# Three edits at the two ends of a fused attention and feed-forward kernel: q's first load in two requests, two constants in one, one store per last tile

## The chip, the cores and the metric

The kernel runs on one core of a Trainium2 chip. The metric is the device time of one launch in microseconds: 280.95 us, the median of 3 runs (280.93 to 281.48). The engines are named as the profile names them: PE is TensorE's matmul stream, PEld its weight loads, DVE is VectorE, ACT is ScalarE, POOL is GpSimd, SP is SyncE. SP, ACT and POOL can issue DMA requests; the requests are carried out by 16 DMA engines that all three share.

## What is computed

Linear attention with cosine weights for 8 batches of 8 heads (576 tokens, 64 features per head), and then a two-layer product with the gate h cos h over all 4608 tokens. From the reference:

```python
r = np.maximum(x, 0.0)                                  # x is q or k
phi = np.concatenate([r * c, r * s], axis=-1)           # c, s: cos and sin of (pi/2) * pos / 576
kv  = np.einsum('bhsf,bhsd->bhfd', k_p, v);  z = np.sum(k_p, axis=2)
num = np.einsum('bhsf,bhfd->bhsd', q_p, kv)
den = np.einsum('bhsf,bhf->bhs', q_p, z)[..., None] + 1e-06
x = (num / den).transpose(0, 2, 1, 3).reshape(4608, 512)
h = x @ w_in                                            # 512 x 2048
g = h * np.cos(h)
out = g @ w_out                                         # 2048 x 512, float32
```

## The kernel before

The 4608 tokens are worked on in nine chunks of 512. Eight batches give 576 tokens each: 512 of them make the batch's own chunk, and the 64 left over of every batch together make the ninth chunk, numbered 8. So the last chunk's four tiles of 128 tokens each hold 64 tokens of an even batch (partitions 0 to 63) and 64 tokens of the odd batch after it (partitions 64 to 127).

Each chunk passes through three stages: attention (load q, k, v; scale by cosines and sines; transpose; products; normalize; transpose), `layer1` (product with `w_in`, cosine, gate) and `layer2` (product with `w_out`, store). From the third chunk on `layer1` can, and `layer2` does, use a scheme of seven half-size products in place of eight, with sums formed on DVE or by DMA. `Plan.add` collects steps with their engine, cost and dependencies. The order is not worked out when the kernel is built: `STARTS` holds one planned time for each step and `ENGS` the engine, and `Plan.run` sorts the steps by the planned time. On each engine the instructions then stand in that order, and a semaphore is waited for wherever data is not there yet.

The parts of the code around the change:

- `setup` (L1025): ACT issues the load of `CS` (cosines and sines, 128 partitions of 24 floats, L1032) and then of `IDENT` (the 128 x 128 identity in float16 that PE uses for its transposes, L1033). `CS` is read by every scaling step (`prep`, L369 and L370), `IDENT` by every transpose on PE.
- `load` (L330): a batch's q, k or v comes in two parts. 320 of the tokens lie as five rows to a partition (`go5`, L337) and 256 as four rows to a partition (`go4`, L340), each on one half of the 128 partitions. SP issues these loads (`LQ`). For the first chunk the order on SP is q (four rows, five rows), k (four, five), and v in two groups of four heads (four, five, four, five). DVE and ACT scale q only after both of its parts have landed.
- `weights` (L1048): POOL copies one element of scaled q and then issues the loads of `w_in`, so that the weights do not run ahead of q, k and v.
- `layer2(8)` (L917), the last stage: sums of the earlier products are stored as they are finished, and the seventh product completes the first 256 output columns of the last two tiles; each tile is added up by DVE (L1020) and stored by `store_tile` (L859).
- `store_tile` calls `put` (L821) twice for a tile, once for each half of the partitions: the half of the even batch goes by SP, the half of the odd batch by ACT. Each request stores 64 rows of 256 floats, 64 KB. Ahead of them each of SP and ACT stores 256 KB and 128 KB of the same chunk.

At the end of the program SP waits for every store to land.

Of the kernel before, what the change touches and what calls it, by code (L numbers as in the profile page):

```python
# [17 lines left out]
OPT = dict(F16=0, WS2=[3, 1], HQ=[3, 0, 1], AQ=0, L0S=0, FW=[20, 4, 4, 4, 4], W2F=2, WQ=3, L2F=0, WFI=None,  # L18
           XPE=[0, 1, 2, 3, 4], FAST1={3: 2, 4: 2, 5: 2, 6: 4, 7: 4, 8: 4}, MODE={}, HH='', LD=[['k', 0],
           ['v', 0], ['q', 0], ['k', 1], ['v', 1], ['q', 1]], NB=[['A0', 'A1'], ['A0', 'A1', 'M0']],  # L20
           XB=[['B3'], ['B3', 'M1']], W0=5, W1=6, WF=[[2, 2, 2, 2], [2, 2, 0, 0]], HOLD=['k', 1], P0=0,
           RAW1=4, WO2=1, H1=0, DA=0, W2=0, SQ=0, NUZ=1)
# [169 lines left out]
def kernel(  # L192
# [12 lines left out]
    P = 128  # L205
# [29 lines left out]
    def sb(name, shape, dt=F16):  # L235
        return pool.tile(shape, dt, name=name)
# [1233 lines left out]
```

## Time and profile before

| what | value |
|---|---|
| median of 3 runs | 280.95 us |
| the profiled execution, whole | 282.01 us |
| span from its first instruction to its last | 280.2 us |
| instructions | 6814 |
| granted TensorE clock | 1.000 throughout |
| DMA, mean over the span | 207 GB/s |

The span is what the rows below count in; the whole time of an execution also holds what lies before and after it. The views used are: the page (busy time of each engine, the chain of waits that ended last as shares), the same chain in order of time, the timeline of instructions and DMA issues, windows (busy time of each engine in a stretch, then TensorE's clock, the share of time in which the 16 DMA engines were busy, and GB/s), the DMA view of a stretch (the share of the DMA engines in tenths and the GB/s for 40 equal slices, then the queues and the issues with the time from issue to landing) and the instructions of one tile. In the DMA view q1 is SP's queue, q10 is ACT's and q0 is POOL's. A line such as "out<-in x4: 497/558/618" gives the least, the median and the longest duration in ns.

### The profile page before, as it was taken

The page shows a single profiled execution, that of the slowest core. Times are in us where ns is not written, and L with a number is a line of the kernel's source. Part 1 is how long each engine was busy: PE and PEld are TensorE (multiplying, and loading weights), DVE is VectorE, ACT ScalarE, POOL GpSimd, SP SyncE. Part 2 cuts the span into 40 slices and gives each one's busy share as a digit, 9 for nine tenths or more (in the row PEclk, how much of TensorE's full clock was granted, in tenths as well). Part 3 has the DMA queues.
Part 4 walks back from the last instruction along what each step waited for, and adds up shares of the span by engine and source line. Part 5 has one row for each costly group of instructions (what it writes and reads, how often), then busy time and mean ns, then how long its engine had stood idle before and what let it go on. Part 6 is the DMA issues. An engine that isn't in the chain of part 4 may idle for free.

```text
span 280.2 us, 6814 instructions
## 1 busy us (share of the span) xinstructions
PE 270.6 (97%) x2689; PEld 213.9 (76%) x2689; DVE 235.3 (84%) x439; ACT 212.4 (76%) x366; POOL 83.5 (30%) x105
## 2 busy tenths in 40 slices
PE   8799999999999999999999999999999999999993
PEld 3468847788866577778777878789988888888882
DVE  1886877999999998999999998989989879873952
ACT  2847698999999896788989988995658686776330
POOL 1360010210602101530340045042534372399210
PEclk9999999999999999999999999999999999999999
DMA  6999999799999999979999998839656495698125
GB/s 201 337 195 204 291 334 310 261 271 191 321 306 244 213 250 266 284 216 227 258 265 271 209 259 282 116 92 147 157 75 144 104 156 107 151 143 123 75 77 150
DMA packets 80223, 58.03 MB, mean 207 GB/s; under 512 B 43200, under 2 KB 77248, under 8 KB 80192
## 3 DMA queue, kind: packets, MB, share of 16 engines
q1 hardware_dynamic: 68960, 39.99, 60.6%
q0 software_dynamic: 10496, 17.04, 29.0%
q10 hardware_dynamic: 736, 0.57, 0.7%
q8 instruction: 21, 0.34, 0.5%
q14 instruction: 10, 0.08, 0.1%
HBM read 36.75 MB, written 11.80 MB: 173 GB/s over the span
## 4 chain that ended last, share of the span: by engine, by line
PE 83%; DVE 7%; DMA 4%; ACT 2%; issue 1%; SPq 0%; DVEq 0%
PE M L956 32%; PE M L737 14%; PE M L576 9%; PE M L609 8%; PE TR L737 6%; PE M L881 3%; PE ATT L465 3%; PE ATT L398 3%; DMA qT<-KQ 2%; DMA qm<-in_q_dram 2%; DVE gT L550 2%; PE TR L609 2%; PE ATT L1044 1%; DVE XN L486 1%; DVE KQ L370 1%
## 5 line engine op out<-in xcount | busy, mean ns | idle before, releaser
L956 PEld LDWEIGHTS <-gT 128*128 128x128 f16 x560 | 53.8, 98 | 7.6
L956 PE MATMUL M<-w_out_sb,gT 128*128 128x256 f16 x448 | 57.0, 273 | 0.0
L550 DVE TENSOR_TENSOR gT<-M,ch 128x512 f16<-128x512 f32 x73 | 48.7, 684 | 5.2 <-ACT ch L548 5.1
L548 ACT ACTIVATE ch<-M 128x512 f32<-128x512 f32 x75 | 43.9, 596 | 12.0 <-PE M L576 6.2
L369 ACT ACTIVATE KQ<-km,CS 128x512 f16<-128x512 f32 x58 | 39.7, 719 | 0.6 <-DMA km<-in_k_dram 0.6
L967 ACT ACTIVATE ost<-M 128x512 f32<-128x512 f32 x41 | 24.4, 597 | 18.0 <-PE M L956 13.0
L369 ACT ACTIVATE KQ<-qm,CS 128x512 f16<-128x512 f32 x48 | 32.8, 718 | 4.5 <-DMA qm<-in_q_dram 4.5
L609 PE MATMUL M<-xT,w_in_sb 128*128 128x512 f16 x136 | 33.6, 379 | 0.0
L956 PE MATMUL M<-T,S 128*128 128x256 f16 x256 | 32.4, 273 | 0.0
L385 POOL CAST V<-vm 128x1024 f16<-128x1024 f32 (+1 forms) x18 | 15.8, 903 | 51.5 <-DMA vm<-in_v_dram 14.7
L737 PEld LDWEIGHTS <-w_in_sb 128*128 128x128 f16 x288 | 27.2, 98 | 4.8 <-issue 0.4
L576 PE MATMUL M<-xT,w_in_sb 128*128 128x256 f16 x256 | 30.1, 272 | 0.8 <-DVE gT L550 0.5
L576 PEld LDWEIGHTS <-w_in_sb 128*128 128x128 f16 x256 | 24.6, 97 | 5.0 <-issue 1.4
L956 PEld LDWEIGHTS <-S 128*128 128x128 f16 x256 | 24.9, 98 | 4.6 <-DVE S L932 0.2
L749 DVE TENSOR_TENSOR Z<-M,Z 128x512 f32<-128x512 f32 x31 | 21.1, 687 | 4.6 <-PE M L737 3.2
L609 PEld LDWEIGHTS <-w_in_sb 128*128 128x128 f16 x160 | 14.9, 98 | 12.4
L550 POOL TENSOR_TENSOR gT<-Z,ch 128x512 f16<-128x512 f32 x5 | 6.3, 1266 | 56.7 <-ACT ch L548 20.0
L486 DVE TENSOR_TENSOR XN<-ATT,rec 128x512 f16<-128x512 f32 x32 | 22.1, 691 | 1.1
L465 PEld LDWEIGHTS <-qT 128*128 128x128 f16 (+1 forms) x320 | 14.7, 101 | 6.0 <-issue 2.7
L745 ACT ACTIVATE Z<-M 128x512 f32<-128x512 f32 x26 | 15.1, 596 | 4.0 <-PE M L737 3.0
L760 ACT ACTIVATE ch<-Z 128x1024 f32<-128x1024 f32 x12 | 12.7, 1057 | 6.9 <-DVE Z L749 4.9
L465 PE MATMUL ATT<-kvz,qT 128*128 128x65 f16 (+1 forms) x288 | 16.1, 195 | 0.9 <-DMA qT<-KQ 0.4
(153 smaller groups left out, 512.6 us busy)
## 6 DMA issues: line engine op xcount, KB each, us to landing
out_dram<-ost POOLq DMA_DIRECT2D x38, 256.0 KB, 4.0
qm<-in_q_dram SPq DMA_DIRECT2D x8, 640.0 KB, 6.2
km<-in_k_dram SPq DMA_DIRECT2D x8, 640.0 KB, 7.1
qm<-in_q_dram SPq DMA_DIRECT2D x8, 512.0 KB, 6.4
km<-in_k_dram SPq DMA_DIRECT2D x8, 512.0 KB, 5.2
vm<-in_v_dram SPq DMA_DIRECT2D x6, 640.0 KB, 6.6
vm<-in_v_dram SPq DMA_DIRECT2D x6, 512.0 KB, 4.8
w_in_sb<-in_moe_w_in_dram POOLq DMA_DIRECT2D x4, 512.0 KB, 7.9
```

The lines of the kernel that those rows point to most:

```text
L369: fn = {"ACT": lambda: nc.scalar.activation(out=out_, in_=in_, func=AF.Relu, scale=sc), "DVE": lambda: nc.vector.tensor_scalar(out=out_, i ...
L385: "POOL": lambda: nc.gpsimd.tensor_copy(out=out_, in_=in_)}
L465: nc.tensor.matmul(bank[hb][ps, hh * D1:(hh + 1) * D1], lhsT=x[:, h, :], rhs=z[:, h, :], start=True, stop=True)
L486: nc.vector.tensor_tensor(out=split(x16[n][:, hs, :], k), in0=A[:, :, :, 0:D], in1=split(rec[n][:, hs], k).unsqueeze(3).broadcast_to((P, k ...
L548: act(0.5, due, lambda: nc.scalar.activation(out=ch[c], in_=bank, func=AF.Sin, bias=math.pi / 2.0, scale=1.0), [key], [("ch", c)])
L550: mul(due, 0.61, lambda q: q.tensor_tensor(out=dst, in0=bank if len(dst.shape) == 2 else bank.rearrange("p (j s) -> p j s", j=dst.shape[1] ...
L576: nc.tensor.matmul(M1[m][:, jj * 2 * P:(jj + 1) * 2 * P], lhsT=w_in_sb[:, cc, j * P:(j + 1) * P], rhs=X[:, cc, ts], start=(cc == 0), stop= ...
L609: nc.tensor.matmul(M, lhsT=w_in_sb[:, cc, j * P:(j + 1) * P], rhs=X[:, cc, :], start=(cc == 0), stop=(cc == NCT - 1))
L737: nc.tensor.matmul(bank[0][:, j * TH:(j + 1) * TH], lhsT=a(cc, j), rhs=b[:, cc, :], start=(first and j == 0 and cc == 0), stop=(last and j ...
L749: dve(0.61, due + 0.3, lambda: nc.vector.tensor_tensor(out=dst, in0=bank[0], in1=dst, op=ALU.add), [bank[1], key], [key])
L956: nc.tensor.matmul(bank[0][:, tt * MH:(tt + 1) * MH], lhsT=a[:, j, tt * P:(tt + 1) * P], rhs=b[:, j, :], start=(first and (apart or tt == ...
L967: act(0.5, due, lambda: nc.scalar.activation(out=dst, in_=view(bank), func=AF.Copy), [bank[1]], dk)
```

## The change

Three edits; the matmuls and the order of everything else on each engine stay as they were, and the planned times are only renumbered.

1. The four-row part of q's first load is issued as two requests of four heads each in place of one of eight heads (`QS`). The five-row part stays one request.
2. `CS` and `IDENT` become views of one tile `CONST` (352 bytes to a partition), filled by one request of ACT.
3. `store_tile` stores a tile by one request for both halves (`TM`): the first tile by ACT, the second by SP.

```diff
-OPT = dict(F16=0, WS2=[3, 1], HQ=[3, 0, 1], AQ=0, L0S=0, FW=[20, 4, 4, 4, 4], W2F=2, WQ=3, L2F=0, WFI=None,
...
+OPT = dict(TM=1, CM=0, QS=1, F16=0, WS2=[3, 1], HQ=[3, 0, 1], AQ=0, L0S=0, FW=[20, 4, 4, 4, 4], W2F=2, WQ=3,
...
-    cs_dr = nc.inline_tensor(cs_np, name="cs_const")
-    ident_dr = nc.inline_tensor(np.eye(P, dtype=np.float16), name="ident_const")
+    CW = cs_np.size // P
+    const_np = np.concatenate([cs_np.reshape(P, -1), np.eye(P, dtype=np.float16).view(np.float32)], axis=1)
+    const_dr = nc.inline_tensor(np.ascontiguousarray(const_np), name="const")
...
-    CS = sb("CS", [P, 2, 2, NT + 2], F32)
-    IDENT = sb("IDENT", [P, P])
+    CONST = sb("CONST", [P, CW + P // 2], F32)
+    CS = CONST[:, 0:CW].rearrange("p (n g t) -> p n g t", n=2, g=2)
+    IDENT = CONST[:, CW:CW + P // 2].bitcast(F16)
...
+            elif b == 0 and nm == "q" and OPT["QS"]:
+                def go4s(h, four):
+                    return lambda: LQ.dma_start(out=blocks(m, 1 - n)[:, h, 0:NT, :], in_=four[:, h])
+                for hs_ in HALVES:
+                    pl.add(LE, LO, 0, due, go4s(hs_, four), (), [(x, 1 - n) for x in part[hs_]],
+                           dma=(nb * NT / 2, 355.0), lane="first", late=LATE_BY[0], lazy=None)
...
     def store_tile(o, i, due):
+        if OPT["TM"]:
+            dst = out.rearrange("(i n s) m -> n i s m", n=2, s=S)[:, 2 + i, 0:S5, 0:MH]
+            put(due, dst.rearrange("n (p t) m -> n p t m", t=NT + 1)[:, :, NT],
+                ost[o][:, i, 0:MH],
+                [("ost", o, 0, i)], *((nc.sync, "SP") if i else (nc.scalar, "ACT")), nb=131.0)
+            return
...
-        nc.scalar.dma_start(out=CS, in_=cs_dr.ap())
-        nc.scalar.dma_start(out=IDENT, in_=ident_dr.ap())
+        nc.scalar.dma_start(out=CONST, in_=const_dr.ap())
```

More of the change, by code (lines that the diff above doesn't have):

```diff
@@ L15 @@
 SYNC = mybir.DependencyInfo(mybir.DependencyClass.Sync, mybir.DependencyReason.DATA)
-OPT = dict(F16=0, WS2=[3, 1], HQ=[3, 0, 1], AQ=0, L0S=0, FW=[20, 4, 4, 4, 4], W2F=2, WQ=3, L2F=0, WFI=None,
[L19 to L22, printed above, removed]
@@ L25 @@
-STARTS = (
[98 rows of a table removed]
+OPT = dict(TM=1, CM=0, QS=1, F16=0, WS2=[3, 1], HQ=[3, 0, 1], AQ=0, L0S=0, FW=[20, 4, 4, 4, 4], W2F=2, WQ=3,
+           L2F=0, WFI=None, XPE=[0, 1, 2, 3, 4], FAST1={3: 2, 4: 2, 5: 2, 6: 4, 7: 4, 8: 4}, MODE={}, HH='',
+           LD=[['k', 0], ['v', 0], ['q', 0], ['k', 1], ['v', 1], ['q', 1]], NB=[['A0', 'A1'], ['A0', 'A1',
+           'M0']], XB=[['B3'], ['B3', 'M1']], W0=5, W1=6, WF=[[2, 2, 2, 2], [2, 2, 0, 0]], HOLD=['k', 1],
+           P0=0, RAW1=4, WO2=1, H1=0, DA=0, W2=0, SQ=0, NUZ=1)
@@ L124 @@
+STARTS = (
[98 rows of a table added]
 )
 ENGS = (
-    "DDPPPPPSSSSSSSSDAPDDDPADAPDDAPAGGGGDADADDDADADADADDADADGGGGGGGPPADPPDPPAPPDPPAPPDPPAPPDP"
-    "APADPADPADPADPADPADPADPADPADPADPADPADPADPADPADPADGSSGSSGGGGGSSSSDADADADADADAPDDAPADAPDDA"
-    "PADADADADDADADPPAPPDPAPPDPAPPDPAPPDPAPDPPDPAPAPAPAPAPDPDGGPDPDGGPADPADPADPADPADPADPADPAD"
-    "PADPADPADPADPADPADPADPADDDDDSSSSSSAADDDADADAGGGPPAAASDDSAASDASPPDPAPPDPAPPDPAPPDPADDDPPA"
-    "PPDDPPAPPAPPDPPDGGPPAGGPADPADPADPADPADPADPADPADPADPADPADPADPADPADPADPADSSSSSSDAAAAAAAAAG"
@@ L131 @@
-    "GGPPAAASAASAASADSAAPPDSPPDSPPDSPPDSSPPDSDDDDDDDPPAPPDDPPAPPAPPDPPDGGPPAGGDDDDPAPDAGPAPAP"
-    "DPDADPADPADPADPADPADPAPDAGPAPAPDPDADPADPADPADPADPADSSSSSSAAAAAAAAAAGGGPPAAASAASAASADSPPD"
-    "SPPDSPPDSPPDSDDDPPAPPDDPPAPPAPPDPPDGGPPAGGDDDDPAPDAGPAPAPDPDADPADPADPADPADPADPAPDADPAPAP"
-    "DPDADPADPADPADPADPADSSSSSSDDAAAAAAADGGGPPAADSAASDDSAASAAPPDSPPDSPPDSPPDSSPPDSDDDPPAPPADP"
-    "PAGGPPAPPAPPAGGPPAGGGGDDDDPAPDAGPAPAPDPDADPADPADPADPADPADPAPDADPAPAPDPDAGPADPADPADPADPAD"
-    "SSSSSSAAAAAAADAAGGGPPAAASADSADSAASPPDSPPDSPPDSPPDSDDDDDDDPPAPPADPPAGGPPAPPAPPAGGPPAGGGGD"
@@ L137 @@
-    "DDDPAPDADPAPAPDPDADPADPAPDAGPAPAPDPDAGPADPAPDADPAPAPDPDADPADPAPDADPAPAPDPDADPADSSSSSSDAA"
-    "AAAAAAAGGGPPADASDASAASDDSAAPPDSPPDSPPDSPPDSSPPDSDDSPPAPPAGGPPAGGPPAPPAPPAGGPPAGGGGDDDDPA"
-    "PDAGPAPAPDPDAGPADPAPDADPAPAPDPDADPADPAPDADPAPAPDPDADPADPAPDADPAPAPDPDADPADDDDDSPPAPPDGGP"
-    "PAPPAPPDPPDGGPPAGGDDDDPAPDAGPAPAPDPDAGPADPAPDAGPAPAPDPDAGPADPAPDAGPAPAPDPDADPADPAPDAGPAP"
-    "APDPDADPADDDDDDDPPAPPDDDPPAPPAPPDPPDSASAAPPDSADSA"
+    "DDPPPPPSSSSSSSSSDAPDDDPADAPDDAPAGGGGDADADDDADADADADDADADGGGGGGGPPADPPDPPAPPDPPAPPDPPAPPD"
@@ new lines @@
+    "PAPADPADPADPADPADPADPADPADPADPADPADPADPADPADPADPADGSSGSSGGGGGSSSSDADADADADADAPDDAPADAPDD"
+    "APADADADADDADADPPAPPDPAPPDPAPPDPAPPDPAPDPPDPAPAPAPAPAPDPDGGPDPDGGPADPADPADPADPADPADPADPA"
+    "DPADPADPADPADPADPADPADPADDDDDSSSSSSAADDDADADAGGGPPAAASDDSAASDASPPDPAPPDPAPPDPAPPDPADDDPP"
+    "APPDDPPAPPAPPDPPDGGPPAGGPADPADPADPADPADPADPADPADPADPADPADPADPADPADPADPADSSSSSSDAAAAAAAAA"
+    "GGGPPAAASAASAASADSAAPPDSPPDSPPDSPPDSSPPDSDDDDDDDPPAPPDDPPAPPAPPDPPDGGPPAGGDDDDPAPDAGPAPA"
+    "PDPDADPADPADPADPADPADPAPDAGPAPAPDPDADPADPADPADPADPADSSSSSSAAAAAAAAAAGGGPPAAASAASAASADSPP"
@@ new lines @@
+    "DSPPDSPPDSPPDSDDDPPAPPDDPPAPPAPPDPPDGGPPAGGDDDDPAPDAGPAPAPDPDADPADPADPADPADPADPAPDADPAPA"
+    "PDPDADPADPADPADPADPADSSSSSSDDAAAAAAADGGGPPAADSAASDDSAASAAPPDSPPDSPPDSPPDSSPPDSDDDPPAPPAD"
+    "PPAGGPPAPPAPPAGGPPAGGGGDDDDPAPDAGPAPAPDPDADPADPADPADPADPADPAPDADPAPAPDPDAGPADPADPADPADPA"
+    "DSSSSSSAAAAAAADAAGGGPPAAASADSADSAASPPDSPPDSPPDSPPDSDDDDDDDPPAPPADPPAGGPPAPPAPPAGGPPAGGGG"
+    "DDDDPAPDADPAPAPDPDADPADPAPDAGPAPAPDPDAGPADPAPDADPAPAPDPDADPADPAPDADPAPAPDPDADPADSSSSSSDA"
+    "AAAAAAAAGGGPPADASDASAASDDSAAPPDSPPDSPPDSPPDSSPPDSDDSPPAPPAGGPPAGGPPAPPAPPAGGPPAGGGGDDDDP"
@@ L142 @@
+    "APDAGPAPAPDPDAGPADPAPDADPAPAPDPDADPADPAPDADPAPAPDPDADPADPAPDADPAPAPDPDADPADDDDDSPPAPPDGG"
+    "PPAPPAPPDPPDGGPPAGGDDDDPAPDAGPAPAPDPDAGPADPAPDAGPAPAPDPDAGPADPAPDAGPAPAPDPDADPADPAPDAGPA"
+    "PAPDPDADPADDDDDDDPPAPPDDDPPAPPAPPDPPDSASAAPPDADS"
 )
```

196 rows, old and new, of the table STARTS are left out of this document.

## The prediction

> **What bounds the kernel now.** I read the page's busy lines first, then the chain of waits at both ends, because the change touches only the first microseconds and the last ones.
>
> ```profile
> span 280.2 us, 6814 instructions
> ...
> PE 270.6 (97%) x2689; PEld 213.9 (76%) x2689; DVE 235.3 (84%) x439; ACT 212.4 (76%) x366; POOL 83.5 (30%) x105
> ...
> PE 83%; DVE 7%; DMA 4%; ACT 2%; issue 1%; SPq 0%; DVEq 0%
> ```
>
> TensorE (PE) carries 83% of the chain, so the middle can be neither shortened nor lengthened by this change; it can only begin earlier or later. The chain in order of time, start and length, at the two ends:
>
> ```profile
> 1.55 5.94 DMA qm<-in_q_dram
> ...
> 7.63 1.29 DVE KQ L370 x3
> ...
> 8.96 1.09 PE M L429 x16
> ...
> 11.81 2.59 PE ATT L1044 x12
> 14.40 1.32 PE M L398 x40
> ...
> 19.93 1.05 PE M L576 x8
> ```
>
> ```profile
> 259.77 13.99 PE M L956 x128
> ...
> 275.14 0.82 DVE ost L1020 x2
> ```
>
> At the start all waits for q: its second request lands at 1.55 + 5.94 = 7.49, DVE scales, PE transposes, and so on up to the first projection at 19.93. At the end the last two additions run from 275.14 to 275.96; what follows up to 280.2 (4.2 us) is stores alone. So two stretches can move: 0 to 7.5 and 276 to 280.
>
> The stages by busy time (the last two columns are the share in which the 16 DMA engines are busy, and GB/s):
>
> ```profile
> 2.25:3.05 0.80, 0.80 (x4) 0.25 (x3) 0.00 (x0) 0.79 (x2) 0.00 (x0) 1.00 0.47 81
> 3.05:7.50 4.45, 4.11 (x17) 1.58 (x15) 0.00 (x0) 0.06 (x1) 0.00 (x0) 1.00 1.00 341
> 7.50:10.80 3.30, 1.83 (x27) 1.59 (x28) 2.77 (x6) 2.97 (x4) 0.66 (x3) 1.00 1.08 360
> 276.20:278.50 2.30, 0.00 (x0) 0.00 (x0) 0.00 (x0) 0.00 (x0) 0.00 (x0) 1.00 0.79 247
> 278.50:280.20 1.70, 0.00 (x0) 0.00 (x0) 0.00 (x0) 0.00 (x0) 0.00 (x0) 1.00 0.00 0
> ```
>
> The load stream is slow until 3.05, then full. One DMA engine carries 360 / 16 = 22.5 GB/s at the full rate; I price with that.
>
> **The first load in halves.** The timeline of the issues (start, length):
>
> ```profile
> 0.74 0.75 SPq L340 DMA_DIRECT2D qm<-in_q_dram  x1
> 0.75 0.35 ACTq L1032 DMA_DIRECT2D CS<-cs_const  x1
> ...
> 1.14 0.44 ACTq L1033 DMA_DIRECT2D IDENT<-ident_const  x1
> ...
> 1.55 0.62 SPq L337 DMA_DIRECT2D qm<-in_q_dram  x1
> ...
> 2.22 0.64 SPq L340 DMA_DIRECT2D km<-in_k_dram  x1
> ...
> 6.10 0.74 SPq L337 DMA_DIRECT2D vm<-in_v_dram  x1
> ```
>
> One request of 512 KB becomes two of 256 KB; the five-row request of q and all six loads of k and v behind it on SP's queue are issued one issue later, about 0.65 us. Cover: the stream still has q's first 512 KB to move, at 341 GB/s 1.54 us, from 3.05 to 4.6. The five-row request would go out at 2.2, and its data can flow some 1.5 later (the first went out at 0.74; its packets are those of the stretch from 2.25), at 3.7. So it is not late; were the cover gone, q would land up to 0.65 later, then k, the transposes and everything to the end. The last v request goes from 6.10 to about 6.75; it now waits for q's first half to have landed, which is before 5.7 (the whole took 4.9 from 0.74), so this wait costs nothing; behind it SP's next load waits 6.5 us for DVE anyway.
>
> ```profile
> qm<-in_q_dram SPq DMA_DIRECT2D x1, 512.0 KB, 4.9
> ```
>
> ```profile
> SPq L340 <- DVE KQ L370: 6.5, 1, 6.5
> ```
>
> The gain: between 2.25 and 3.05 the stream ran at 81 of 341 GB/s, a loss of 0.8 x (1 - 81/341) = 0.61 us. Should this be the time in which one large request is spread, halving it saves 0.3; should it be a fixed start-up, 0. I take 0.15.
>
> **The constants as one load.** ACT issues once and is free 0.44 earlier, which is worth nothing: its next real work waits for q, as DVE's does. The identity's packets now run between q's; in the stretch from 3.05 to 5.5:
>
> ```profile
> q10 hardware_dynamic: 144, 0.03, 6.2%
> ```
>
> 6.2% of 2.45 us is 0.15 us of all 16 engines. Joined to the cosines they move before 2.3, when the engines idle. It is hidden if the new load lands before 7.5; the cosines took 1.7 and the identity 3.8 from issue, so it does. Gain 0.15, bounds 0 and 0.15.
>
> ```profile
> IDENT<-ident_const ACTq DMA_DIRECT2D x1, 32.0 KB, 3.8
> CS<-cs_const ACTq DMA_DIRECT2D x1, 12.0 KB, 1.7
> ```
>
> k and v ride in the same stream, so they land earlier by as much as q, and ACT, the only engine that waited for k, waited 0.2 us: no second wait holds the gain back.
>
> ```profile
>   DMA km<-in_k_dram: 0.2, 1
> ```
>
> Start: -0.3, bounds -0.45 and +0.65.
>
> **The last stores.** Before, each 128-token tile goes out as two requests, SP's half and ACT's half, each written 64 x 256: 64 rows of 1 KB. After, one request of ACT for tile 0 and one of SP for tile 1. SP no longer issues for tile 0, so tile 1 goes out when its addition ends, 276.0 instead of 276.2.
>
> ```profile
> L822 SPq DMA_DIRECT2D out_dram<-ost x2: 497/558/618, 275.6 to 276.2; - x2
> L822 ACTq DMA_DIRECT2D out_dram<-ost x2: 513/655/797, 275.6 to 276.2; - x2
> ...
> DMA to landing us min/median/max: 2.6/2.7/2.9
> ```
>
> The last of the four lands at 276.2 + 2.7 = 278.9; the end comes 1.3 later. SP's four stores begin at 272.82, the second, of 128 KB, at 274.51; it and ACT's of 128 KB landed 3.4 and 3.6 later:
>
> ```profile
> 272.82 3.98 SPq L822 DMA_DIRECT2D out_dram<-ost  x4
> ```
>
> ```profile
> 274.51 1.58 SPq L822 DMA_DIRECT2D out_dram<-ost  x2
> ```
>
> ```profile
> out_dram<-ost SPq DMA_DIRECT2D x1, 128.0 KB, 3.4
> out_dram<-ost ACTq DMA_DIRECT2D x1, 128.0 KB, 3.6
> ```
>
> What the diff does not say is in the built program: the new request is written 2 x 64 x 256 on the output's side, because the two halves of a tile lie in two different batches and no single step covers both. Its first count is 2, against 128 partitions on the other side. Every plain request of SP and ACT before has 64 or 128 as its first count on both sides. No row shows a request with a small first count, so I bound it. If it is spread over 16 engines as now, the 256 KB take 262,144 B / 360 GB/s = 0.73 us, and the end gains up to 0.2. If it is cut along its first count, it has two shares, and two engines carry 64 KB per request. With both requests on the same pair, each engine moves 131,072 B / 22.5 GB/s = 5.83 us, while 14 engines stand idle.
>
> I take two engines: the count of 64 that becomes 2 is what the change alters in these stores besides their number, and no other equal cut fits a pattern of 2 on one side and 128 on the other without splitting a step. When do the two engines begin? Not before 276.9: data flowed 1.3 us after the store issued at 272.82 (slices of 0.1 us from 272.8; the first is in slice 14):
>
> ```profile
> DMA  0000000000000799979999698898899989467676
> ```
>
> Not after 277.6, when the 128 KB pair is out (it lands by 278.1; the last data of all, moved by 278.4, landed 0.5 later). I take 277.0: of that pair each engine has only 16 KB, 0.73 us. Then the data ends at 277.0 + 5.8 = 282.8 and lands at 283.3 to 283.4 instead of 278.9: +4.5; by the two starts +4.3 to +5.0. SP's wait for the stores, 1.9 us now, is the wait that grows:
>
> ```profile
> SPq L1465 <- DMA out_dram<-ost: 1.9, 1, 1.9
> ```
>
> The rate has bounds too. At 28 GB/s (the best slices of the load stream, 456 GB/s over 16, in the stretch from 3.05) it is 4.6 us, +3.3; at 19.5 (247 GB/s at a share of 0.79 over 16, the tail's own row) 6.7 us, +5.4.
>
> ```profile
> GB/s 201 251 234 334 351 322 368 347 305 305 276 322 280 272 314 330 351 355 339 318 314 347 310 255 334 326 330 293 180 280 242 280 222 234 263 426 456 372 355 355
> ```
>
> The Trainium skill, page "DMA: Bandwidth & Descriptors", section "Why a DMA increments its semaphore by 16 and not by 1", says that the queue takes the slowest dimension that is not 1 on both sides and uses the largest number of engines, up to 16, that divides both; for 2 and 128 that is two engines, on SP's and ACT's requests the lowest-numbered ones, so both stores would share a pair. No run here shows it yet. By that page's other rule, that transfers are best batched into few large ones (section "Bandwidth"), the merge should help; the sum would then be the 16-engine case.
>
> **Sum.** -0.3 at the start, +4.5 at the end: +4.2. The profiled execution took 282.01 us around its span of 280.2; the median of the runs is 280.95, and I put the sum on that: 285.1, with the span near 284.4.
>
> **The rivals.**
> (1) Sixteen engines still. For it: 64 and 128 rows are spread over all engines now, and the number of rows is unchanged. Against it: the pattern itself. The end gains 0 to 0.2 and the start 0.3: 280.95 - 0.4 = 280.5. It decides from the point where the landing of the last two stores stays under 3 us.
> (2) Two engines, but another pair for each store. Then tile 1, issued at 276.0, flows from 277.3 for 65,536 B / 22.5 GB/s = 2.9 us to 280.2 and lands at 280.7: +1.8, minus 0.3: 282.4. For it: the two stores stand on two queues. Against it: the two queues share the 16 engines, and nothing says that they begin at different ones.
> (3) The late issue on SP costs what I said is covered, 0.5 at the start instead of a gain, on top of the slow stores: 285.9. For it: the slow stretch before 3.05 may belong to each new request. Against it: later requests, back to back, run at 341 and more.
> That the constants or the halves do nothing at all only takes the 0.3 away.
>
> **How the numbers follow.** Forecast 0.73, rival (1) 0.13, (2) 0.08, (3) 0.06. 0.2% (0.56 us) is about what a measurement of this kernel can tell from no change. The forecast, (2) and (3) are all slower by more: 0.87. Rival (1) lies at -0.45, mostly inside 0.56: 0.08 no change, 0.05 faster. The forecast's own range is 283.9 (the fast rate) to 286.9 (the slow rate, with the 0.5 of (3)). The range for 8 in 10 reaches down to (2): 282.2 to 287.0.
>
> **What would show it.** The two last stores land 5 us or more after issue instead of 2.6 to 2.9; DMA share near 0.13 (2 of 16) at about 45 GB/s from 277.6 to 283; the last addition ends near 275.7; q lands near 7.2; the identity's packets are gone from the stretch after 3.05. Wrong is the forecast if the DMA engines are done by 278.5 as now, and its start term if q lands after 7.5.

## The result: slower by 2.5%, more than forecast at both ends

| | before | after |
|---|---|---|
| median of the runs | 280.94 us (280.65 to 281.48, 6 runs) | 287.68 us (287.16 to 289.2, 6 runs) |
| the profiled execution, whole | 282.01 us | 287.16 us |
| its span | 280.2 us | 285.3 us |

The ratio after to before is 1.0248, 95% interval 1.0216 to 1.0279: 6.1 to 7.8 us more. The forecast was 285.1 us, 4.15 above 280.95.

The page of the kernel after, its span, busy lines and the chain of waits by engine and by line:

```profile
span 285.3 us, 6812 instructions
...
PE 271.3 (95%) x2689; PEld 214.2 (75%) x2689; DVE 235.2 (82%) x439; ACT 212.3 (74%) x366; POOL 83.5 (29%) x105
...
PE 87%; DVE 5%; DMA 2%; ACT 1%; issue 1%; SPq 0%; DVEq 0%
```

PE does the same 2689 matmuls in 271.3 us where it took 270.6; its share falls only because the span is longer. The time came in where PE does nothing, at the two ends.

**The start.** The chain of waits of the kernel after in order of time (start, length):

```profile
0.74 0.78 SPq L350
...
1.58 0.62 SPq L350
...
2.24 6.21 DMA qm<-in_q_dram
...
8.58 1.29 DVE KQ L378 x3
...
20.88 1.04 PE M L584 x8
```

The chain now goes through both halves' issues, and q's five-row request, issued at 2.24, lands at 8.45 where it landed at 7.49. DVE's scaling and the first projection are each 0.95 later. The windows of the two kernels show the stretch in which that happened; first before, then after (the last two columns are the DMA engines' share and GB/s):

```profile
3.05:4.50 1.45, 1.45 (x6) 0.60 (x5) 0.00 (x0) 0.06 (x1) 0.00 (x0) 1.00 0.94 310
4.50:7.50 3.00, 2.66 (x13) 0.98 (x11) 0.00 (x0) 0.00 (x0) 0.00 (x0) 1.00 1.02 356
```

```profile
2.25:3.05 0.80, 0.80 (x4) 0.25 (x3) 0.00 (x0) 0.37 (x2) 0.00 (x0) 1.00 0.64 117
3.05:4.50 1.45, 1.45 (x5) 0.56 (x4) 0.00 (x0) 0.00 (x0) 0.00 (x0) 1.00 1.02 334
4.50:7.50 3.00, 3.00 (x10) 1.14 (x9) 0.00 (x0) 0.00 (x0) 0.00 (x0) 1.00 0.93 292
```

Up to 4.5 the change is ahead: 117 GB/s where 81 were, then 334 against 310. From 4.5 to 7.5, when the five-row request is served, it runs at 292 against 356, though the DMA engines count as busy for 0.93 of the time. The loss is largest at the beginning of that stretch; the same half microsecond before and after:

```profile
4.50:5.00 0.50, 0.50 (x4) 0.20 (x3) 0.00 (x0) 0.00 (x0) 0.00 (x0) 1.00 0.94 277
```

```profile
4.50:5.00 0.50, 0.50 (x2) 0.15 (x1) 0.00 (x0) 0.00 (x0) 0.00 (x0) 1.00 0.68 169
```

So it is a partial hole where the four-row data gives way to the five-row data, and a stretch behind it that is less than full.

**The tail.** The kernel after, DVE's last additions in the timeline, the two merged stores among the forms of the storing line (least, median, longest issue in ns, first and last start), and two windows:

```profile
275.09 0.82 DVE L1034 TENSOR_TENSOR ost<-M,ost 128x256 f32<-128x256 f32 x2 [0.66 <-ACT ost L981]
```

```profile
L830 SPq DMA_DIRECT2D out_dram<-ost x3: 618/619/664, 272.8 to 275.5; - x3
L830 ACTq DMA_DIRECT2D out_dram<-ost x3: 637/750/1067, 272.8 to 276.0; - x3
```

```profile
277.50:278.80 1.30, 0.00 (x0) 0.00 (x0) 0.00 (x0) 0.00 (x0) 0.00 (x0) 1.00 0.10 9
278.80:284.00 5.20, 0.00 (x0) 0.00 (x0) 0.00 (x0) 0.00 (x0) 0.00 (x0) 0.59 0.14 48
```

The additions start 0.05 earlier than before (275.09 against 275.14), so the whole middle is no later, though it began 0.95 later; more on that below. From their start to the end of the span it was 280.2 - 275.14 = 5.1 us and is 285.3 - 275.09 = 10.2. For 5.2 us the last data moves at 48 GB/s with 0.14 of the 16 DMA engines busy: two engines, 24 GB/s each. Ahead of that lie 1.3 us with 9 GB/s. The DMA view names the queue. From 278.8 to 280.5 only SP's store moves, from 282 to 284 only ACT's, each at the rate of two engines:

```profile
q1 hardware_dynamic: 80, 0.08, 13.5%
```

```profile
q10 hardware_dynamic: 95, 0.10, 13.7%
```

So the two stores stand behind each other on one pair. The wait of SP at the end of the program, 1.9 us before, has grown, as the waits of SP's queue show (in all, times, longest):

```profile
SPq L1478 <- DMA out_dram<-ost: 7.8, 5, 3.2
```

**What hides in the middle.** The profiled execution of before has a pause in its chain that the one of after has not:

```profile
100.54 6.51 DMA qT<-KQ
```

The share "DMA qT<-KQ 2%" of before's page is gone from the page of after. Up to there after is 0.95 behind, and behind it level. `qT` is the transposed q of a later chunk. Such a pause isn't peculiar to either kernel: of the fifteen executions profiled for this document, nine have one or two of them in their chain, of changed and unchanged starts alike. This execution's 282.01 us lie 1.07 above the median. Whoever compares the two profiled executions alone, 287.16 - 282.01 = 5.15, misses the start's loss; the medians, 6.7 apart, do not.

### The profile page after: what moved, and what is told of

Read it like the earlier page. It is cut to its first block, busy times and chain, and to the rows that moved or that the text cites. A ratio compares the mean times of both kernels' runs of the same rounds, so it can differ in the third digit from the quotient of the medians.

```text
span 285.3 us, 6812 instructions
## 1 busy us (share of the span) xinstructions
PE 271.3 (95%) x2689; PEld 214.2 (75%) x2689; DVE 235.2 (82%) x439; ACT 212.3 (74%) x366; POOL 83.5 (29%) x105
## 4 chain that ended last, share of the span: by engine, by line
PE 87%; DVE 5%; DMA 2%; ACT 1%; issue 1%; SPq 0%; DVEq 0%
PE M L970 34%; PE M L745 14%; PE M L617 10%; PE M L584 9%; PE TR L745 6%; PE M L895 3%; PE ATT L406 3%; PE ATT L473 3%; DMA qm<-in_q_dram 2%; PE TR L617 2%; PE ATT L1057 1%; DVE KQ L378 1%; PE M L437 1%; DVE gT L558 1%; DVE XN L494 1%
## 5 line engine op out<-in xcount | busy, mean ns | idle before, releaser
L377 ACT ACTIVATE KQ<-km,CONST 128x512 f16<-128x512 f32 x58 | 39.7, 720 | 0.5 <-DMA km<-in_k_dram 0.5
L377 ACT ACTIVATE KQ<-qm,CONST 128x512 f16<-128x512 f32 x48 | 32.8, 718 | 6.1 <-DMA qm<-in_q_dram 6.1
L843 POOL DMA_DIRECT2D out_dram<-ost x12 | 13.3, 1202 | 11.1 <-ACT ost L981 11.1
```

The lines of the kernel that those rows point to most:

```text
L377: fn = {"ACT": lambda: nc.scalar.activation(out=out_, in_=in_, func=AF.Relu, scale=sc), "DVE": lambda: nc.vector.tensor_scalar(out=out_, i ...
```

## The experiments

Each kernel is the one before with the edit shown. Each ratio is to runs of the kernel before taken beside it, whose medians were 281.23 to 281.85 us. The theory behind the first four, A: the two ends add up, and each has its own cause.

**The tail alone.**

```diff
+            if i in (0, 1):
+                both = out.rearrange("(i n s) m -> n i s m", n=2, s=S)[:, 2 + i, 0:S5, 0:MH]
+                both = both.rearrange("n (p t) m -> n p t m", t=NT + 1)[:, :, NT]
...
+                    lambda q=q, both=both: q.dma_start(out=both, in_=ost[o][:, i, 0:MH])
```

> Only the third edit: each of the last two tiles stored by one request, written 2 x 64 x 256; q's load and the constants as before. Theory A (the two ends add up: two DMA engines at the end cost 5.1 us, the start of the change 0.95 to 1.6): 286.0, the last two stores at about 48 GB/s in all and a DMA share of 0.13, q landing at 7.5. Theory B (the start's loss was that one execution's, all of the 6.7 us is the end's): 287.6. Theory C (sixteen engines): 280.9.

Measured: 287.66 us (286.49 to 288.05, 4 runs), ratio 1.0212, 1.0170 to 1.0254. Its timeline has the additions at 274.41, and its span is 284.7: 10.3 us, as in the full change.

```profile
274.41 0.82 DVE L1026 TENSOR_TENSOR ost<-M,ost 128x256 f32<-128x256 f32 x2 [0.66 <-ACT ost L973]
```

So the tail is worth 5.2 us in the profiles, 4.8 to 7.1 by the runs, and it is by far the larger part. The median is the number of theory B and not the 286.0 of theory A. The next run decides between them: the start costs time by itself.

**The start alone; the halves alone; the constants alone.**

```diff
+    LQ.dma_start(out=blocks(m, 1 - n)[:, 0:HB, 0:NT, :], in_=four[:, 0:HB])    # halves
+    LQ.dma_start(out=blocks(m, 1 - n)[:, HB:H, 0:NT, :], in_=four[:, HB:H])
...
+    nc.scalar.dma_start(out=CONST, in_=const_dr.ap())                          # constants
```

Both edits:

> The first two edits without the third: q's four-row load in two requests and the constants as one load; four stores of 64 rows at the end as before. Theory A: 281.9 to 282.5, q landing at 8.3 or later and the first projection near 20.9. Theory B: 280.9, q landing at 7.5. My forecast's start term was -0.3: 280.6.

The halves:

> Only q's four-row load in two requests; constants and stores as before. If the start's loss comes from the split or the later issues on SP: 281.9 to 282.5 with q landing at 8.3 or later. If it comes from the constants: 280.9, q landing at 7.5.

The constants:

> Only the constants as one load; q's load and the stores as before. If the start's loss comes from the constants: 281.9 to 282.5 with q landing at 8.3 or later. If from the split: 280.8, q landing at 7.35 (0.15 us of the identity's packets gone from between q's).

Measured: both 283.17 us (281.76 to 284.83, 10 runs), ratio 1.0060, 1.0031 to 1.0088; halves 284.36 (283.83 to 285.03, 5 runs), ratio 1.0097, 1.0065 to 1.0129; constants 280.82 (280.44 to 283.34, 10 runs), ratio 0.9993, 0.9964 to 1.0022. The chains of the three, in this order:

```profile
2.25 5.85 DMA qm<-in_q_dram
...
90.95 7.35 DMA qT<-KQ
101.26 6.90 DMA qT<-KQ
```

```profile
2.23 7.26 DMA qm<-in_q_dram
```

```profile
1.57 5.38 DMA qm<-in_q_dram
```

q lands at 8.10, 9.49 and 6.95. Theory B, that the start costs nothing, is out (1.0060, interval above 1); the first two medians lie above the 281.9 to 282.5 of theory A. By the ratios the ends make 2.1% and 0.6%, together 2.7%, where the whole change made 2.2 to 2.8%. The loss at the start is that of the halves; the constants cost nothing and gain nothing that these runs can tell. The halves' stream is slow in the same stretch as after, only more so:

```profile
4.50:7.50 3.00, 3.00 (x13) 1.19 (x11) 0.00 (x0) 0.00 (x0) 0.00 (x0) 1.00 0.86 242
```

The halves alone lose more than q's lateness. q is 2.0 late in this execution, but the first projection starts at 23.50, 3.57 later than before. PE had been idle for 3.2 us, and soon after it went on its granted clock (the first of the last three columns) was halved for 3.4 us:

```profile
12.30:15.30 3.00, 3.00 (x17) 1.74 (x15) 2.91 (x7) 2.78 (x5) 1.82 (x2) 0.50 0.81 218
```

The execution with the delay alone, next, shows the same after 3.7 us of idle PE (0.50 from 11.3 to 14.3, first projection 3.54 later); the full change and both edits, with 1.5 and 1.2 us idle, do not.

Halves do two things at once: they make the first request smaller and they send the five-row request out one issue, some 0.65 us, later. The next runs separate these.

**The lateness without the halves.** q's first load is whole; behind it SP issues a load of 12 KB that nobody reads.

```diff
+    LQ.dma_start(out=blocks(m, 1 - n)[:, h, 0:NT, :], in_=four)
+    LQ.dma_start(out=ost[2][:, 0, 0:24], in_=cs_dr.ap().rearrange("p a b c -> p (a b c)"))
```

> Edit: the kernel before, q's first load whole, and a load of 12 KB (a second copy of the cosines, into a store buffer that is not yet in use) put on SP's queue between q's two loads. So q's five-row request is issued one issue (some 0.65 us) later without any split. Lateness theory (the start is lost because the five-row request goes out late): q's last landing at 8.1 or later instead of 7.49, first projection 0.6 us or more later than 19.93, median +0.6 to +3, 281.8 to 284. Split theory (the loss comes from the two half-size requests themselves): q's landing at 7.4 to 7.7, median within 0.5 of 281.

Measured: 283.25 us (281.74 to 284.75, 10 runs), ratio 1.0071, 1.0044 to 1.0098. Chain and window:

```profile
2.21 7.29 DMA qm<-in_q_dram
```

```profile
4.50:8.00 3.50, 2.75 (x13) 1.07 (x11) 0.00 (x0) 0.00 (x0) 0.00 (x0) 1.00 0.90 249
```

Without any split the five-row request, issued at 2.21 in place of 1.55, lands at 9.50, and the stream shows the same slow stretch, 249 GB/s with the engines busy. Lateness is enough. (At 284.74 us this execution was one of the two longest of its ten.)

**The halves without the lateness.** In the first of two ways ACT issues the second half:

```diff
+    first.append(lambda: nc.scalar.dma_start(out=blocks(m, 1 - n)[:, HB:H, 0:NT, :], in_=four[:, HB:H]))
```

> Edit: the kernel before, q's four-row load in halves, the first half issued by SP and the second by ACT ahead of its cosines, so that SP's five-row request goes out as early as in the kernel before. Lateness theory: q's last landing at 7.5 or before, median within 0.5 of 281 or a little under it. Split theory: q's landing at 8.3 or later as with both halves on SP (9.49), median 282.5 to 284.5.

Measured: 281.73 us (280.39 to 284.67, 10 runs), ratio 1.0004, 0.9985 to 1.0022. The time is level with the kernel before, as the lateness theory has it (the median itself lies 0.2 above the range that was expected). The profiled execution is not as expected: q landed at 8.21 in it.

```profile
1.56 6.65 DMA qm<-in_q_dram
```

That execution took 283.64 us, 1.9 above the median of its own runs, so its landing need not be that of the usual run. But it shows that q can land late though the five-row request goes out on time. The second way is cleaner. Both halves go on SP, the constants are one load, and ACT issues q's five-row load:

```diff
+    first.append(lambda: nc.scalar.dma_start(out=blocks(m, n)[:, 0:H], in_=five))
```

> Edit: the kernel before with both parts of the change at its start (q's four-row load in halves on SP, constants in one load), and q's five-row load given to ACT ahead of the constants, so that it goes out at once and is not behind the second half. Lateness theory (the start is lost because q's five-row request goes out at 2.2 instead of 1.55 and its stream is reached too soon after): q's last landing at 7.5 or before, median within 0.6 of 281.2, some 2 under the 283.17 of the same edits with the five-row load on SP. Rival (the halves cost by themselves): q's landing at 8 or later, median 282.5 or more.

Measured: 281.27 us (280.66 to 282.38, 10 runs), ratio 1.0000, 0.9984 to 1.0016. Chain and window:

```profile
1.56 5.60 DMA qm<-in_q_dram
```

```profile
4.50:7.50 3.00, 2.71 (x13) 1.03 (x11) 0.14 (x1) 0.17 (x1) 0.00 (x0) 1.00 1.10 362
```

The halves are still there, issued by SP as in the change; q lands at 7.16 and the stream is full. This is the start of the change with one instruction on another queue, and its loss is gone. So halves as such cost nothing in the median; they cost where the five-row request stands behind them on SP's queue. The edit also lets the five rows be served first (they landed at 5.7, the halves after them), so it doesn't separate the lateness from the order.

**An extra request further back.** q's five-row load in two halves instead; the second half goes out at 2.23.

```diff
+    LQ.dma_start(out=blocks(m, n)[:, 0:HB], in_=five[:, 0:HB])
+    LQ.dma_start(out=blocks(m, n)[:, HB:H], in_=five[:, HB:H])
```

> Edit: the kernel before, q's four-row load whole, its five-row load in halves on SP instead (so the first half of it goes out on time and the second, with k and v behind it, one issue late). Lateness theory: the second half is late as the five-row request was, q's last landing at 8.0 or later, median +0.5 to +3, 281.5 to 284. Split theory (an extra request in the stream costs by itself, wherever it stands): about the same, 282 to 284. If only the early place of the extra request matters (the rows behind it are held up while three requests open at once): q's landing at 7.5 or before, median within 0.5 of 281.

Measured: 281.28 us (280.68 to 283.41, 10 runs), ratio 0.9990, 0.9965 to 1.0014.

```profile
2.23 5.62 DMA qm<-in_q_dram
```

```profile
4.50:7.50 3.00, 3.00 (x13) 1.12 (x11) 0.00 (x0) 0.00 (x0) 0.00 (x0) 1.00 1.03 345
```

A request that is issued at 2.23 isn't harmed as such: this one has 320 KB more in front of it, the stream stays at 345 GB/s, q lands at 7.85, between the two landings expected, and the time is that of before. The plain lateness theory had this wrong. The runs so far suggest that what hurts is a request whose turn in the stream comes soon after its issue.

**Twice the lateness.** Two loads of 12 KB ahead of the five-row request.

> Edit: as with the one dummy load of 12 KB ahead of q's five-row load on SP, but two of them, so that the request is some 1.3 us later than in the kernel before. Lateness theory with a threshold that is already passed: each further 0.65 us costs at least 0.65, q's landing at 9.5 or later where one dummy gave 9.50 and the median 283.25, median 283.5 to 285.5. If one dummy's loss was chance in the stream and not its delay: median near 281 to 283, q's landing anywhere between 7.5 and 9.5.

Measured: 282.53 us (281.49 to 284.49, 10 runs), ratio 1.0038, 1.0010 to 1.0066; the expectation was 283.5 at least. Chain, then the DMA view of 0 to 12 in 40 slices of 0.3 us:

```profile
2.67 5.11 DMA qm<-in_q_dram
```

```profile
GB/s 0 0 0 0 0 9 32 69 167 89 229 315 343 377 306 200 111 38 115 346 397 393 367 369 391 389 382 380 344 372 354 358 380 358 354 356 355 359 350 352
```

Issued at 2.67, later than in any other run, the request lands at 7.78, earlier than with one dummy. Here the stream does have a hole: from 4.8 to 5.7 it runs at 111, 38 and 115 GB/s, a loss of 0.9 x (1 - 88/356) = 0.7 us, and then at 346 to 397. So the price doesn't grow with the delay, as the expectation had it. The two landings are no fair pair, though: the profiled execution took 0.5 less than its median here and 1.5 more with one dummy, and the intervals of the two ratios overlap.

**What a busy but slow engine does.** The trace also keeps every packet that a DMA engine moved, with its duration; no view lists them. A packet of q, k or v is one row, 1,024 or 1,280 bytes, and takes 0.05 us as a rule. Some take ten times as long, and they count as busy. For SP's packets that started from 4.0 to 7.5:

| kernel | q landed | packets over 0.2 us | their time in all |
|---|---|---|---|
| five rows on ACT, halves on SP | 7.16 | 0 | 0 us |
| before | 7.49 | 4 | 1.6 us |
| two dummies | 7.78 | 12 | 5.2 us |
| five rows in halves | 7.85 | 14 | 4.7 us |
| both start edits | 8.10 | 19 | 7.3 us |
| halves on two queues | 8.21 | 16 | 8.3 us |
| after | 8.45 | 18 | 7.0 us |
| halves alone | 9.49 | 26 | 11.4 us |
| one dummy | 9.50 | 22 | 9.8 us |

By and large, the later q lands, the more time lies in such packets. The five-row data itself did begin in time: its first packet starts at 4.12 in the change and at 4.38 before. Why single packets take so long, and why more of them do after a late issue, stays open.

**Both parts of q at once.** Constants in one load, q's four rows on SP and its five rows on ACT, both at 0.74.

> Edit: the kernel before, constants in one load, q's four-row load whole on SP and its five-row load on ACT ahead of the constants, so that both go out at 0.75 and k 0.65 earlier than before. Lateness theory, carried on: an earlier five-row request can only help, and it has two queues opening side by side; q's last landing at 6.3 to 7.0, median 0.5 to 1.0 under the kernel before, 280.2 to 280.7. If an early five-row request is worth nothing beyond not being late (the stream itself is the limit): median within 0.4 of 281.2. If ACT's constants, now behind 640 KB in the same queue, hold the first scaling up: q is not the last to land, the first projection is later than 19.9 and the median 281.8 or more.

Measured: 281.24 us (280.71 to 282.52, 12 runs), ratio 0.9994, 0.9979 to 1.0009. Its issues from 0 to 12 (KB, us to landing), and its chain:

```profile
qm<-in_q_dram ACTq DMA_DIRECT2D x1, 640.0 KB, 6.1
...
qm<-in_q_dram SPq DMA_DIRECT2D x1, 512.0 KB, 6.3
```

```profile
1.32 7.41 PE ATT L1050 x20
8.73 1.08 PE M L436 x16
```

q is complete by 0.74 + 6.3 = 7.04, and it is no longer in the chain: twenty opening matmuls of PE that wait for no load (fillers on a constant tile, `warm`, L1040 of the kernel before) end at 8.73, and the transposes start there, where before they started at 8.96. In the profiled execution of before the same twenty took less, as its timeline shows:

```profile
1.32 5.84 PE L1044 MATMUL ATT<-S 128*128 128x512 f16 x20 [1.32 <-POOL S L1026]
```

The difference is the pace of each one. From 4.3 to about 7.2 the same matmul took 388 ns in before and 629 ns here (the second number after the bar):

```profile
L1044 PE MATMUL ATT<-S 128*128 128x512 f16 x14 | 3.3, 388 | 0.0
```

```profile
L1050 PE MATMUL ATT<-S 128*128 128x512 f16 x8 | 3.6, 629 | 0.0
```

Every one of them is slow at first, and the quick ones begin at 4.2 in before and at 7.3 here; the trace's record of the full clock begins at 4.09 and at 7.26. That moment differs between executions, also of the unchanged start; why, stays open. Where they take 7.41, a faster load of q gains no more than 8.96 - 8.73 = 0.23, and the medians show no gain at all.

**One merged store in place of two.** Tile 0 by one request of ACT, tile 1 by two as before; shown against the kernel with the tail alone.

```diff
-            if i in (0, 1):
+            if i in (0,):
```

> Edit: the kernel before, only token tile 0 of the last product stored by one request (ACT's), tile 1 still by two. One pair of engines for both stores (my theory): the pair now has 64 KB in all for each engine, half of what both stores gave it, 65,536 B / 24 GB/s = 2.7 us instead of 5.5, so the end of the span is 2 to 3 us later than before (before ends 5.0 after the last product's PE work, both merged 10.2), median 283 to 284. Another pair for each store (rival): each pair has the same work as with both merged, the end stays 5 us late, median 286 to 287.7.

Measured: 284.62 us (284.45 to 285.87, 4 runs), ratio 1.0125, 1.0093 to 1.0157, 2.6 to 4.4 us more. The median is above the 283 to 284 that the theory of one pair gave, and further below the 286 that the rival needed. The merged store in the forms of its line, and three windows:

```profile
L869 ACTq DMA_DIRECT2D out_dram<-ost x1: 1164/1164/1164, 275.0 to 275.0; - x1
```

```profile
277.00:278.30 1.30, 0.00 (x0) 0.00 (x0) 0.00 (x0) 0.00 (x0) 0.00 (x0) 0.50 0.12 24
278.30:279.60 1.30, 0.00 (x0) 0.00 (x0) 0.00 (x0) 0.00 (x0) 0.00 (x0) 0.50 0.13 46
279.60:281.00 1.40, 0.00 (x0) 0.00 (x0) 0.00 (x0) 0.00 (x0) 0.00 (x0) 0.50 0.08 28
```

Two engines move 128 KB at 24, then 46, then 28 GB/s: the rates of one engine, two, and one again. Read so, each carries its 64 KB in some 2.6 us, the second beginning 1.3 after the first; that the two are staggered is read from the rates, since the trace names no engine. One store costs more than half of both (3.4 by the medians, 6.4 with both) because the stagger is paid in either case, and less than both because in the change the two stores stand behind each other on the same two engines. With a pair for each store, the two would have run at twice 48 GB/s while both were under way.

**Merged the other way.** As many bytes and requests as in the change, but one request per half of the partitions, with both tiles in it, so that 64 rows come first.

```diff
+    dst = out.rearrange("(i n s) m -> n i s m", n=2, s=S)[n][2:4, 0:S5, 0:MH]
+    dst = dst.rearrange("i (p t) m -> p t i m", t=NT + 1)[:, NT]
+    q.dma_start(out=dst, in_=ost[o][n * R:(n + 1) * R, 0:2, 0:MH])
```

In a first run the requests went out after tile 1's addition, which DVE does first, so tile 0 was stored without its last addition; its end can't be compared. The timeline has that addition waiting for the store:

```profile
279.58 0.42 DVE L1025 TENSOR_TENSOR ost<-M,ost 128x256 f32<-128x256 f32 x1 [3.58 <-DMA out_dram<-ost]
```

> Edit: the kernel before, the last product's four stores of 64 KB made two of 128 KB as in the change, but merged the other way: one request per half (SP's rows of one batch, ACT's of the other), both token tiles in it, written 64 x 2 x 256, after the second addition. As many bytes and requests as in the change, with 64 and not 2 as the first count. First-count theory (mine: the request is cut along its first count, so 2 gives two engines): the share of the DMA engines stays near 0.8 until the data is out, landing within 3 us of issue, median within 0.5 of 281.2. Rival (128 KB in one request at the very end, or waiting for both additions, is what costs): landing 4 us or more after issue, median 284 or more.

```profile
276.20:278.50 2.30, 0.00 (x0) 0.00 (x0) 0.00 (x0) 0.00 (x0) 0.00 (x0) 1.00 0.85 257
```

The window shows the rate, 0.85 of the engines at 257 GB/s. Measured: 282.03 us (281.09 to 282.94, 10 runs), ratio 1.0014, 0.9997 to 1.0031, a little above the median expected. The second run issues after both additions.

> Edit: the kernel before, the last product's four stores of 64 KB made two of 128 KB, merged the other way than in the change: one request per half, both token tiles in it, written 64 x 2 x 256, and issued when both additions are done (in the run before this one the request went out after tile 1's addition, and tile 0's came behind it). First-count theory: 0.8 or more of the DMA engines busy until the data is out, landing within 3.6 us of issue as the 128 KB pair of the kernel before, so some 0.5 later than before in all, median 280.9 to 282.0. Rival (two large requests at the very end cost by themselves): landing 4.5 us or more after issue, median 284 or more.

Measured: 281.69 us (280.44 to 283.29, 12 runs), ratio 0.9993, 0.9964 to 1.0021. The additions in the timeline, the stores' landing, and a window:

```profile
274.18 0.82 DVE L1025 TENSOR_TENSOR ost<-M,ost 128x256 f32<-128x256 f32 x2 [0.66 <-ACT ost L972]
```

```profile
DMA to landing us min/median/max: 3.0/3.1/3.2
```

```profile
274.90:277.20 2.30, 0.00 (x0) 0.00 (x0) 0.10 (x1) 0.00 (x0) 0.00 (x0) 1.00 0.85 254
```

From the additions to the end of the span (279.2) it is 5.0 us, as before the change. Two requests of 128 KB at the very end cost nothing when their first count is 64. The cause of the tail is the first count of 2, not the merging: bytes, number of requests and row length are the same in both.

## Why the prediction was wrong, step by step

**Right: where time can move, and the sign of the whole.** PE does the same work in the middle, the tail is stores alone, and the change is slower. The sign of the start was wrong: it lost time where the forecast had it gain 0.3.

**Right: two engines, one pair, their rate.** The forecast took 22.5 GB/s for an engine and 5.83 us for the data; 24 GB/s and 5.2 us were measured at 0.14 of 16 engines. The Trainium skill, page "DMA: Bandwidth & Descriptors", section "Why a DMA increments its semaphore by 16 and not by 1", gave two engines for a pattern whose slowest counts are 2 and 128; the share of 0.13 to 0.14 agrees, and the run merged the other way, with 64 first, shows 0.85. The sixteen-engine rival falls with it, and so does the rival of a pair for each store. The forecast let tile 0 go first; DVE adds tile 1 first, and SP's store goes out at 275.5, ACT's at 276.0, which changes nothing.

**Mis-sized: when the two engines begin.** The forecast took 277.0, with 277.6 as the latest, because the 128 KB pair ahead would be out by then. It was out by 277.5, but for another 1.3 us the merged requests moved at 9 GB/s, and the full two-engine rate began at 278.8. Data ended at 284.0 instead of 282.8. The end of the span followed 1.3 later, where the forecast allowed for the landing and then 1.3. Net: +5.15 instead of +4.5. The forecast's bound for the beginning was too early because it held the merged request's own opening to that of a plain store, 1.3 us after issue; ACT's issue alone took 1.07 us, against 0.64 and 0.75 for its others (SP's merged one took no longer than its others, 0.62 to 0.66), and the rates of the single merged store fit two engines that begin 1.3 apart. The trace's packets show the slow opening: between 277.6 and 278.8 four rows of 1 KB took 0.36 to 0.49 us each, and from 278.6 on each takes 0.046.

**Wrong, and the step that failed: "So it is not late."** The forecast worked out that the five-row request could flow at 3.7 while the four-row data lasted until 4.6, and it priced an extra gain of 0.3 for the start. The first data was in fact not late (4.12). The forecast took the moment from which a request can deliver its first data for the moment from which it delivers at the full rate. Sent 0.65 later, it was served at 292 GB/s in place of 356 from 4.5 to 7.5, and q was 0.95 late. The run with a delay and no halves shows the same; the run with the halves on SP and the five rows on ACT does not; one execution with the halves on two queues does, so lateness isn't the only way to it. Counted from the issue to 4.6, where the forecast let the four-row data end, the request had 3.05 us before the change and 2.4 after it. The second half of the five-row load, also issued at 2.23 but with 320 KB more in front of it (0.9 us at 356 GB/s), had 3.3 and was served in full. That is no rule: with two dummies the request had 1.9 and its data, after a hole, came at the full rate. The third rival had the place right, at a price of 0.5 and with a chance of 0.06. The start costs 0.95 in the profile and 0.9 to 2.5 by the runs of the two start edits.

**The gains can't be told.** The halves did bring data earlier (117 against 81 GB/s before 3.05), and the constants were hidden as worked out (they landed 1.9 us after issue). With the constants alone q landed at 6.95, but the first projection began only 0.27 earlier (19.66), and an interval of 0.3% to either side, 0.8 us, hides the forecast's 0.15. In the run with both parts of q at once, q complete at 7.04 moved the transposes only from 8.96 to 8.73, since PE's twenty opening matmuls ended there. The forecast said nothing of that floor.

**The v loads.** The last of SP's v requests was forecast for about 6.75 without cost; the timeline has it at 6.76, and no wait in the chain comes from it.

```profile
6.76 0.93 SPq L339 DMA_DIRECT2D vm<-in_v_dram  x1
```

**The sum.** +5.15 and +0.95 make 6.1 in place of 4.2. On the median of before that is 287.0, against 287.16 for the profiled execution and 287.68 for the median. What is left, 0.6, lies inside the intervals of the two ends' own runs (4.8 to 7.1 and 0.9 to 2.5). In the profile of the start's edits alone the chain has two pauses at `qT`, where before has one and after none, so a later start can also meet the middle differently; that was not followed further. A start late enough can lose more, by the halved clock that the halves alone and one dummy show; whether runs of the full change meet it is not known, its profiled execution doesn't.

No version beat the kernel before: the constants alone (0.9993), q on two queues (0.9994), the five rows in halves (0.9990) and the stores merged by half (0.9993) are all even with it.

## What to carry to other kernels

When two stores or loads are merged, look in the built program at the first count of the pattern that results, and merge along a dimension that leaves the many rows in front; here the same two requests cost 5 us or nothing by that alone. When a request is put in front of another on an issuing queue, don't take the first data of the next one for its full rate: ask how long after its issue its turn in the stream comes, or give one of them to an idle queue, which here took the loss away (1.0060 to 1.0000). Before pricing an earlier load, find what else its first user waits for. Compare medians of many runs before two profiled executions: a pause of the middle hid the start's whole loss here.

## What the hardware showed unexpectedly

A request that was 0.65 us late had the load stream slow for 3 us in one execution (249 GB/s with 0.90 of the engines counted as busy), while one that was 1.1 late left a hole and cost no more (1.0038 against 1.0071, with intervals that overlap). Busy engines were slow because single packets of about 1 KB took 0.2 to 1.3 us where 0.05 is the rule; a share of busy time near 1 doesn't show that a stream is at its rate.

A store cut in two shares moved 9 GB/s for its first 1.3 us and 48 from then on. Alone, its rates fit engines that begin 1.3 us apart. It kept ACT 1.07 to 1.16 us at its issue, and SP 0.61.

After 3.2 and 3.7 us of idle PE the granted clock was 0.50 for 3.4 us; after 1.5 us it stayed at 1.00.
